# Weights in the free parts of the last inputs' tiles, a tenth pair in another order, and one unit of token products behind the last sum

## The chip, the cores and the metric

The kernel runs on one core of one Trainium2 chip. The metric is the device time of one execution in microseconds (us); the median of three runs stands for the kernel.

## What is computed

Two layers follow each other. The first is linear attention with a decay: for each of 4 batches and 8 heads a 64x64 state is decayed and added to at each of 768 positions. Its output, 3072 tokens of 512 numbers, goes into a soft mixture of experts: 32 slots take a softmax-weighted mean of all tokens, 8 experts of 4 slots each run two matrix products, and each token takes a softmax-weighted mean of the 32 slot outputs.

```python
for t in range(S):
    state = gamma * state + einsum('bhd,bhe->bhde', k[:, :, t], v[:, :, t])
    y[:, :, t] = scale * einsum('bhd,bhde->bhe', q[:, :, t], state)
x = y as 3072 tokens x 512
logits = x @ phi                                   # phi 512 x 32
slot_input = softmax(logits over tokens).T @ x     # 32 x 512, 4 slots per expert
h = maximum(slot_input[e] @ w1[e], 0)              # w1[e] 512 x 1024
slot_out[e] = h @ w2[e]                            # w2[e] 1024 x 512
out = softmax(logits over slots) @ slot_out        # 3072 x 512
```

All numbers are float32. w1 and w2 are 16 MB each (1 MB here is 1024 KB), the inputs q, k, v 18 MB, the output 6 MB.

## The kernel before

**Stages.** The attention runs in 24 steps, a step being 128 positions of one batch with all 8 heads, and the steps go in 12 pairs P = 0 to 11 (steps 2P and 2P + 1). In a pair TensorE does these in order: the part of the output that comes from the state (`carry_mm`, L251), the part from within the step (`attend_mm`, L260, with the masked scores as an operand), the state's update (`state_mm`, L288), the turning of the output into token order (`natural_mm`, L304), and the scores of the next pair (`score_mm`, L227). After each come copies or masks out of PSUM on ScalarE and VectorE (`attend_copy`, L276 to L280; `natural_copy`, L311; `score_mask`, L235). GpSimd decays q and v of the next pair (`decay_q`, L212; `decay_v`, L217). Every second pair closes a group of four steps, whose logits and softmax sums are folded into the pooled slot inputs; `turn_mm` (L364) and `turn_copy` (L369) are part of that.

Then `hidden` (L607) multiplies the slot inputs with the 16 tiles of w1 in the order of the table `weights`, and the last loop (L687) sums the products with w2 in three blocks of output columns, 256, 128 and 128 wide, in 16 units each. A block's sum is finished by the generator `finish`: a copy of the sum to SBUF (`os_`, L652), a product that repeats it for four row groups (L656), a copy of that (`s4`, L657), and then the token products in units of 64 columns: four products (L668), four copies on VectorE and ScalarE in turn (L673), one store of 768 KB (L674). The block of 256 has four such units, the others two each. `finish` is advanced by one `yield` per unit of the next block; the tables Y1, Y2 and BURST say how many yields stand before and between its parts.

**Queues and order.** Every engine runs its instructions in the order of the code. All loads and stores are issued by SyncE (SP): an issue waits until the buffer that it fills has been read for the last time, and what stands behind it in the code waits with it. Every eighth DMA shares a semaphore lane, so an issue also waits until the one eight before it has landed.

**Buffers.** Tiles of 1 MB come from two pools: `big` (13) for weights and `inp` (6) for the inputs of six steps. A step's tile holds kT, qT, v and k in natural order, 512 columns of the 2048 each. Steps in LEAN load only the first three (768 KB) and make the fourth on TensorE where it is wanted; the last four steps, 20 to 23, don't want it, since no state follows them. `load_in(2P + 6)` and `(2P + 7)` are issued in pair P, so the last inputs (22, 23) are issued in pair 8. PACE gives the number of weight tiles issued in each pair: 13 up to P = 8, which fills `big`; two in P = 10 and two in P = 11, which go into the tiles of steps 18 to 21 once those are done. In P = 11 follow the first half tile of w2 in a slot of `ring` and a second in `sst` (the state), and two tiles in those of steps 22 and 23. Four more halves go to the ring, and the last ten tiles take the place of w1 tiles that `hidden` has used.

Of the kernel before, what the change touches and what calls it, by code (L numbers as in the profile page):

```python
# [34 lines left out]
BURST = (3, 3, 3)  # L35
BLOCKS = [(0, 256), (256, 128), (384, 128)]
Y1 = (3, 3, 1)
Y2 = (4, 4, 1)
# [6 lines left out]
PACE = (1, 1, 1, 2, 1, 2, 1, 2, 2, 0, 2, 2)  # L45
# [36 lines left out]
def retention_soft_moe_kernel(  # L82
# [5 lines left out]
    w2: bass.AP,  # L88
    first_: bass.AP,
# [57 lines left out]
    weights = [("w1", hf, g, k) for hf in range(2) for g in range(2) for k in range(NK)]  # L147
    weights += [("w2", 0, e, hf) for hf in range(2) for e in range(0, NE, 2)]
    weights += [("w2", cb, e, 0) for cb in (1, 2) for e in range(0, NE, 2)]

    def halves_of(cb, e, hf):
        if cb == 0:
            return [[(e + h, 4 * hf + f) for f in range(4)] for h in range(2)]
        return [[(e + h, fc) for fc in range(NFC)] for h in range(2)]

    def load_weights(n):
        for _ in range(n):
            if not weights:
                return
            which, *at = weights.pop(0)  # L160
            t = large(weight_pool[0])
            if which == "w1":
                nc.sync.dma_start(t, w1[tuple(at)])
                w1t[tuple(at)] = t
            else:
                nc.sync.dma_start(t, w2[w2n[0]])
                w2n[0] += 1
                take(at, [t[:, 0:1024], t[:, 1024:2048]])

    def take(at, tiles):  # L170
        w = BLOCKS[at[0]][1]
        for t, fcs in zip(tiles, halves_of(*at)):
            for x, (e, fc) in enumerate(fcs):
                w2t[e, at[0], fc] = t[:, x * w:(x + 1) * w]

    def load_halves(n, first_half=None):
        for _ in range(n):
            _, *at = weights.pop(0)
            tiles = [first_half if first_half is not None else slot(), slot()]
            for h in (1, 0):  # L180
                nc.sync.dma_start(tiles[h], w2[w2n[0], :, h * 1024:(h + 1) * 1024])
            take(at, tiles)
            w2n[0] += 1
# [4 lines left out]
    def load_in(i):  # L188
        t = large(inp)
        st[i] = dict(kT=t[:, 0:512].rearrange("p (g t) -> p g t", t=C),  # L190
# [170 lines left out]
    def turn_mm(g):  # L361
        q = gs[g]
        q["tp"] = bank("sm", (128, C))
        nc.tensor.transpose(q["tp"], q["pT"], ident)  # L364
# [100 lines left out]
    for P in range(NPP):  # L465
        last = P == NPP - 1
        g = P // 2
        load_weights(PACE[P])
        if 2 * P + NIN < NSTEP:
# [42 lines left out]
        if 2 * P + 2 in TURNED:  # L512
            turn_k(2 * P + 2, "A0")
        natural_mm(P)
# [13 lines left out]
        if P == NPP - 2:  # L528
            logits_bank(NGRP - 1)
# [8 lines left out]
        if P % 2 == 0 and 0 < P < NPP - 2:  # L538
# [12 lines left out]
    load_halves(1)  # L551
# [17 lines left out]
    load_halves(1)  # L569
# [34 lines left out]
    def hidden(hf, g, k):  # L604
        for j in range(4):
            a = g * NK * SIW + k * SIW + 4 * j
            nc.tensor.matmul(hp[hf][32 * j:32 * j + 32, :], si0[:, a:a + NSLOT],  # L607
                             w1t[hf, g, k][:, j * 512:(j + 1) * 512],
# [18 lines left out]
    for hf in range(2):  # L627
        for g2 in range(2):
            for k in range(NK):
                hidden(hf, g2, k)  # L630
                load_weights(1)
# [9 lines left out]
    load_weights(len(weights))  # L641

    co_tags = [["sm", "A2", "Y1", "A3", "S", "A0", "Y0"], ["sm", "A2", "Y1", "A3", "S", "A1", "Y0"]]
    last_tags = ["S", "sm", "A2", "Y1", "A3", "A1", "A0", "Y0"]
    pend = []
    n_co = [0]

    def finish(cb, op):
# [11 lines left out]
        for m in range(w // 128):  # L660
            for h in range(2):
                ot = large(big)[:, 0:12 * C].rearrange("p (c j t) -> p c j t", j=B, t=C)
                cps = []
                for j in range(B):
                    tags = co_tags[cb] if cb < len(BLOCKS) - 1 else last_tags
                    cp = bank(tags[n_co[0] % len(tags)]).rearrange("p (c t) -> p c t", t=C)[:, 0:3]
                    n_co[0] += 1
                    nc.tensor.matmul(cp, s4[32 * j:32 * j + 32, m * 128:(m + 1) * 128],  # L668
                                     cT[32 * j:32 * j + 32, 3 * h:3 * h + 3, :], start=True, stop=True,
                                     skip_group_check=True, tile_position=(32 * j, 0))  # L670
                    cps.append(cp)
                for j in range(B):
                    (nc.scalar.copy if j % 2 else nc.vector.tensor_copy)(ot[:, :, j, :], cps[j])  # L673
                nc.sync.dma_start(out[c0 + m * 128:c0 + (m + 1) * 128, h * 12 * C:(h + 1) * 12 * C],  # L674
                                  ot.rearrange("p c j t -> p (c j t)"))
                for _ in range(BURST[cb]):
                    yield

    for cb, (c0, w) in enumerate(BLOCKS):
        if cb == len(BLOCKS) - 1:  # L680
            n_co[0] = 0
# [13 lines left out]
        next(done)  # L695
        for f in pend:
# [7 lines left out]
def lay_out(q, k, v, moe_phi, moe_w1, moe_w2):  # L704
# [16 lines left out]
    for cb, (c0, w) in enumerate(BLOCKS):  # L721
# [3 lines left out]
        else:  # L725
            x = x.reshape(NE // 2, 2, NFC, 128, w).transpose(0, 3, 1, 2, 4)
        w2.append(x.reshape(-1, 128, 2 * FF))
    kt, qt, vn = tr(k), tr(q), nat(v)
    x = np.concatenate([kt, qt, vn, nat(k)], axis=2)
    return dict(x3=x[LEAN][:, :, 0:1536], x4=x[FULL],  # L730
                w1=w1, w2=np.concatenate(w2),
# [24 lines left out]
```

## Time and profile before

| | us |
|---|---|
| median of 3 runs | 158.79 (158.37 to 158.86) |
| profiled execution, its device time | 159.76 |
| its span, first to last instruction | 158.1 |
| TensorE busy in it | 143.1 |
| VectorE, GpSimd, ScalarE busy | 77.6, 58.3, 43.9 |
| read from and written to HBM | 55.05 MB and 6.29 MB (of 10^6 bytes) |

The profiled execution took 159.76 us, 1.7 more than its span; the shown runs without a profile have a median of 158.79. TensorE's granted clock was 1.00 of full speed up to 152 us. The time axis of all rows starts with the span.

### The profile page before, as it was taken

Reading aid. Unit: us, or ns where it says so; the run is one execution under the profiler, and the core shown is the slowest. Engines: PE = TensorE matmul, PEld = TensorE weight load, DVE = VectorE, ACT = ScalarE, POOL = GpSimd, SP = SyncE. Lnnn points to the kernel's source line nnn. Section 1 sums busy time; section 2 is a strip of 40 time slices with the busy share of each in tenths; the row PEclk is TensorE's granted clock in tenths of the full one; section 3 lists DMA queues with packets and bytes.
Section 4 is the critical chain, followed back from the end, with each engine's and each line's share of the span. In section 5 each row is a group of like instructions: output and inputs, shape, how many; then the busy total and the mean of one; then the engine's idle time right before and its main releaser. Section 6 shows DMA issues by size and latency. Waiting matters only on the chain.

```text
span 158.1 us, 5523 instructions
## 1 busy us (share of the span) xinstructions
PE 143.1 (91%) x2424; PEld 106.8 (68%) x2424; DVE 77.6 (49%) x187; ACT 43.9 (28%) x104; POOL 58.3 (37%) x67
## 2 busy tenths in 40 slices
PE   7989999999999798999989997999999999998400
PEld 2769999997999587997979796865333565556200
DVE  0349517483847376574937583766410103545500
ACT  3212452415062303423142205150500001423400
POOL 1352798686838059911994093001100000000000
PEclk9999999999999999999999999999999999999975
DMA  4999999999999999999999978989999999999992
GB/s 174 349 418 435 416 417 418 411 426 417 417 412 419 417 409 424 390 423 417 409 426 401 326 311 309 411 286 424 417 430 413 423 423 419 415 407 421 422 418 95
DMA packets 9816, 61.70 MB, mean 390 GB/s; under 512 B 1088, under 2 KB 1088, under 8 KB 4928
## 3 DMA queue, kind: packets, MB, share of 16 engines
q1 hardware_dynamic: 9792, 61.35, 95.2%
q8 instruction: 19, 0.31, 0.8%
q14 instruction: 5, 0.04, 0.1%
HBM read 55.05 MB, written 6.29 MB: 388 GB/s over the span
## 4 chain that ended last, share of the span: by engine, by line
PE 83%; DMA 5%; POOL 2%; DVE 2%; issue 1%; SPq 1%; ACT 1%; DVEq 0%; ACTq 0%
PE A L227 13%; PE Y L260 13%; PE A L687 9%; PE A L304 7%; PE S L288 6%; PE Y L251 6%; DMA b<-in_x_dram 5%; PE Y L607 4%; PE A L607 4%; PE sm L328 3%; PE A L206 3%; PE S L384 3%; PE S L668 2%; POOL b L212 2%; PE A L668 2%
## 5 line engine op out<-in xcount | busy, mean ns | idle before, releaser
L235 DVE TENSOR_TENSOR r<-A,mi 128x512 f32<-128x512 f32 (+1 forms) x50 | 30.1, 661 | 23.9 <-PE A L227 23.9
L212 POOL TENSOR_TENSOR b<-b,qtab 128x512 f32<-128x512 f32 x20 | 25.3, 1277 | 9.3 <-DMA b<-in_x_dram 4.2
L227 PE MATMUL A<-b 64*128 64x128 f32 x384 | 25.7, 283 | 0.7 <-DMA b<-in_x_dram 0.6
L227 PEld LDWEIGHTS A<-b 64*128 64x128 f32 x384 | 23.0, 191 | 3.9 <-issue 1.7
L217 POOL TENSOR_TENSOR b<-b,kt 128x512 f32<-128x512 f32 x23 | 23.7, 1048 | 3.6 <-DMA b<-in_x_dram 3.6
L260 PE MATMUL Y<-r,b 128*64 128x128 f32 x352 | 21.9, 276 | 0.7 <-POOL b L212 0.7
L260 PEld LDWEIGHTS Y<-r,b 128*64 128x64 f32 x352 | 19.0, 137 | 2.7 <-issue 1.7
L430 POOL TENSOR_TENSOR cn<-cn,cz 128x128 f32<-128x128 f32 x6 | 2.4, 400 | 36.6 <-DVE zc L404 18.5
L687 PE MATMUL A<-b,r 128*32 128x128 f32 (+1 forms) x336 | 14.6, 301 | 0.1
L687 PEld LDWEIGHTS A<-b,r 128*32 128x32 f32 x336 | 9.4, 109 | 6.7 <-issue 4.4
L311 ACT COPY r<-A 128x512 f32<-128x512 f32 x23 | 12.5, 595 | 5.2 <-PE A L304 5.2
L304 PE MATMUL A<-mi,r 128*128 128x128 f32 x96 | 12.9, 276 | 0.8 <-ACT r L279 0.8
L288 PE MATMUL S<-b 128*64 128x64 f32 x304 | 11.1, 222 | 1.3 <-issue 1.3
L304 PEld LDWEIGHTS A<-mi,r 128*128 128x128 f32 x96 | 10.6, 141 | 1.7 <-ACT r L279 1.1
L288 PEld LDWEIGHTS S<-b 128*64 128x64 f32 x304 | 10.4, 138 | 1.6 <-issue 1.6
L251 PE MATMUL Y<-b,sst 64*64 64x128 f32 x304 | 10.6, 276 | 0.0
L280 DVE COPY r<-Y 128x512 f32<-128x512 f32 x9 | 6.2, 691 | 5.9 <-PE Y L260 5.1
L251 PEld LDWEIGHTS Y<-b,sst 64*64 64x64 f32 x304 | 8.2, 132 | 1.2
L297 DVE TENSOR_TENSOR sst<-sst,S 128x256 f32<-128x256 f32 x16 | 6.0, 417 | 3.5 <-PE S L288 3.5
L673 ACT COPY b<-A 128x384 f32<-128x384 f32 x8 | 3.7, 484 | 14.4 <-PE A L668 12.8
L607 PE MATMUL Y<-b,qtab 128*32 128x512 f32 x64 | 7.3, 594 | 0.0
L351 ACT ACTIVATE pT<-sm,nm 128x128 f32<-128x128 f32 x4 | 1.5, 368 | 20.8 <-PE Y L260 10.5
(143 smaller groups left out, 184.0 us busy)
## 6 DMA issues: line engine op xcount, KB each, us to landing
b<-in_w_dram SPq DMA_DIRECT2D x29, 1024.0 KB, 13.3
b<-in_x_dram SPq DMA_DIRECT2D x14, 768.0 KB, 9.3
b<-in_x_dram SPq DMA_DIRECT2D x9, 1024.0 KB, 10.4
out_dram<-b SPq DMA_DIRECT2D x8, 768.0 KB, 9.0
r<-in_w_dram SPq DMA_DIRECT2D x5, 512.0 KB, 9.8
b<-in_first_dram SPq DMA_DIRECT2D x1, 512.0 KB, 3.4
r<-in_first_dram SPq DMA_DIRECT2D x1, 512.0 KB, 4.3
sst<-in_w_dram SPq DMA_DIRECT2D x1, 512.0 KB, 5.7
```

The costliest lines, as they stand in the source:

```text
L212: nc.gpsimd.tensor_tensor(q, q, qtab, ALU.mult)
L217: nc.gpsimd.tensor_tensor(v, v, vsc[:, i // B, a:b].unsqueeze(2).broadcast_to([128, b - a, D]), ALU.mult)
L227: nc.tensor.matmul(s["sc"][r][:, g, :], s["kT"][half(r), g, :], s["qT"][half(r), g, :], start=True, stop=True, skip_group_check=True)
L235: nc.vector.tensor_tensor(s["A"][:, r, g:g + n], s["sc"][r][:, g:g + n], mask.unsqueeze(1).broadcast_to([128, n, C]), ALU.mult)
L251: nc.tensor.matmul(p["y"][k][b][half(half_of(r, g)), gl, :], sst[(2 * P + k) % B][half(r), g, :], s["qT"][half(r), g, :], start=(gl == 0 a ...
L260: nc.tensor.matmul(pr[P]["y"][k][g // 2][half(half_of(r, g)), g % 2, :], s["v"][:, 2 * g + r, :], s["A"][:, r, g, :], start=(P < B // 2 an ...
L288: nc.tensor.matmul(S_[half(r), k, g, :], s["kn"][:, 2 * g + r, :], s["v"][:, 2 * g + r, :], start=True, stop=True, skip_group_check=True)
L304: nc.tensor.transpose(X[k][:, g * 128:(g + 1) * 128], pr[P]["yT"][:, k, g, :], ident)
L311: (nc.scalar.copy if engines[k] == "scalar" else nc.vector.tensor_copy)(xn, pr[P]["X"][k])
L607: nc.tensor.matmul(hp[hf][32 * j:32 * j + 32, :], si0[:, a:a + NSLOT], w1t[hf, g, k][:, j * 512:(j + 1) * 512], start=(g == 0 and k == 0), ...
L668: nc.tensor.matmul(cp, s4[32 * j:32 * j + 32, m * 128:(m + 1) * 128], cT[32 * j:32 * j + 32, 3 * h:3 * h + 3, :], start=True, stop=True, s ...
L687: nc.tensor.matmul(op[32 * j:32 * j + 32, :w], hT[fc // 4][:, fc % 4, 4 * g + j, :], w2t[4 * g + j, cb, fc], start=(n == 0), stop=(n == le ...
```

## The change

It does four things. First, each of the last four steps' tiles gets a quarter of another kind: the columns 1536 to 2047, unused in these steps, are loaded with 256 KB of w2 (`wq`) right behind the step's own input. Second, the first three quarters of the same four tiles are filled with w2 (`wl`, 768 KB each) after the step is done, in the place where whole tiles were loaded. w2's first 4 MB are laid out in HBM for that; the sixteenth tile of w1 comes in two halves, one into a ring slot in P = 10, the other into `sst`. The bytes are the same as before. Third, pair 10 has an order of its own: the scores of step 22 come ahead of `turn_mm` and `natural_mm`, which use other PSUM banks. Fourth, the second unit of token products of the second block (column block 1) is no longer worked off in the third block's loop; its products come after the third block's sum, behind that sum's repeating product, and its copies behind the copy `s4`.

```diff
-BURST = (3, 3, 3)
+BURST = (3, NFC * 2, 1)
+HELD = (1, 1)
-Y1 = (3, 3, 1)
-Y2 = (4, 4, 1)
+Y1 = (3, 3, 2)
+Y2 = (4, 4, 2)
-PACE = (1, 1, 1, 2, 1, 2, 1, 2, 2, 0, 2, 2)
+PACE = (1, 1, 1, 2, 1, 2, 1, 2, 2, 0, 2, 0)
...
+    def load_last_w1(h, t):
+        nc.sync.dma_start(t, w1[1, 1, NK - 1, :, h * 1024:(h + 1) * 1024])
+        w1t.setdefault((1, 1, NK - 1), []).extend(t[:, j * 512:(j + 1) * 512] for j in range(2))
+
+    def load_behind(i):
+        m = i - (NSTEP - B)
+        t = st[i]["tile"][:, 0:1536]
+        nc.sync.dma_start(t, wl[m])
+        take(early[8 + 6 * m:14 + 6 * m], t)
...
         elif i in LEAN:
             nc.sync.dma_start(t[:, 0:1536], in3[LEAN.index(i)])
+            if i >= NSTEP - B:
+                m = i - (NSTEP - B)
+                nc.sync.dma_start(t[:, 1536:2048], wq[m])
+                take(early[2 * m:2 * m + 2], t[:, 1536:2048])
...
         load_weights(PACE[P])
+        if P == NPP - 2:
+            load_last_w1(0, slot())
+        if last:
+            load_behind(2 * P - 2)
+            load_behind(2 * P - 1)
...
         carry_mm(P)
         if last:
-            load_halves(1, sall)
-            load_weights(2)
+            load_last_w1(1, sall)
         attend_mm(P)
         if last:
+            load_behind(2 * P)
+            load_behind(2 * P + 1)
             break
...
+        if P == NPP - 2:
+            score_mm(2 * P + 2)
+            score_mask(2 * P + 2)
+            turn_mm(g - 1, "A2")
+            turn_copy(g - 1)
+            natural_mm(P, names=("S", "sm"))
+            natural_copy(P)
+            logits_bank(NGRP - 1)
+            score_mm(2 * P + 3)
+            score_mask(2 * P + 3)
+            continue
...
+            if (cb, u) == HELD:
+                yield
+            for j in range(B):
+                (nc.scalar.copy if j % 2 else nc.vector.tensor_copy)(ot[:, :, j, :], cps[j])
...
         done = finish(cb, op)
         next(done)
+        if cb == len(BLOCKS) - 1:
+            next(pend[0])
+            next(done)
         for f in pend:
             for _ in f:
                 pass
```

SP's queue behind the input of step 20 stood like this before; x3 are inputs (steps 21, 22, 23), w1 and w2 weights, b a tile of 1 MB, r a ring slot:

```order
L199 DMA b_1055<-in_x3_dram 128x1536
L163 DMA b_1205<-in_w1_dram 128x2048
L163 DMA b_1207<-in_w1_dram 128x2048
L199 DMA b_1209<-in_x3_dram 128x1536
L199 DMA b_1211<-in_x3_dram 128x1536
L163 DMA b_1463<-in_w1_dram 128x2048
L163 DMA b_1465<-in_w1_dram 128x2048
L163 DMA b_1553<-in_w1_dram 128x2048
L166 DMA b_1555<-in_w2_dram 128x2048
L181 DMA r_1577<-in_w2_dram 128x1024
L181 DMA sst_81<-in_w2_dram 128x1024
```

The same place now, from the first quarter of w2 on:

```order
L213 DMA b_1053<-in_wq_dram 128x512
L210 DMA b_1056<-in_x3_dram 128x1536
L213 DMA b_1056<-in_wq_dram 128x512
L170 DMA b_1207<-in_w1_dram 128x2048
L170 DMA b_1209<-in_w1_dram 128x2048
L210 DMA b_1211<-in_x3_dram 128x1536
L213 DMA b_1211<-in_wq_dram 128x512
L210 DMA b_1214<-in_x3_dram 128x1536
L213 DMA b_1214<-in_wq_dram 128x512
L170 DMA b_1467<-in_w1_dram 128x2048
L170 DMA b_1469<-in_w1_dram 128x2048
L187 DMA r_1471<-in_w1_dram 128x1024
```

Four quarters (1 MB) and one half tile (0.5 MB) moved ahead of the first issue that needs the tile of step 20 or 21; SP issues 74 DMAs and branches where it had 70.

TensorE at the end of pair 10, from the last attend products on, before (b_1209 is step 22, b_1211 step 23):

```order
L260 MATMUL Y1_1472<-r_1447,b_1055 64x128 x4
L304 MATMUL A2_1508<-mi_75,r_1505 128x128 x4
L304 MATMUL A3_1513<-mi_75,r_1505 128x128 x4
L364 MATMUL sm_1521<-mi_75,pT_1450 128x128
L227 MATMUL A0_1527<-b_1209 128x128
L227 MATMUL A1_1528<-b_1209 128x128
```

The same place now (b_1211 is step 22, b_1214 step 23):

```order
L275 MATMUL Y1_1478<-r_1451,b_1056 64x128 x4
L242 MATMUL A0_1514<-b_1211 128x128
L242 MATMUL A1_1515<-b_1211 128x128
...
L379 MATMUL A2_1527<-mi_75,pT_1454 128x128
L319 MATMUL S_1531<-mi_75,r_1511 128x128 x4
L319 MATMUL sm_1536<-mi_75,r_1511 128x128 x4
L242 MATMUL A2_1546<-b_1214 128x128
L242 MATMUL A3_1547<-b_1214 128x128
```

The scores of step 22 stand where the turning products of pair 10 stood, which read the copied output of that pair.

TensorE at the third block, before: the last 12 products of its first half, the second unit of block 1 (S, A_2083, Y_2085, sm), the second half, the repeating product, the first unit of block 2:

```order
L687 MATMUL A_2030<-b,r 32x128 x12
L668 MATMUL S<-cT,r 128x384
L668 MATMUL A_2083<-cT,r 128x384
L668 MATMUL Y_2085<-cT,r 128x384
L668 MATMUL sm<-cT,r 128x384
L687 MATMUL A_2030<-b,r 32x128 x32
L656 MATMUL Y_2129<-os,rep 128x128
L668 MATMUL S<-cT,r 128x384
```

The same place now; S, A_2121, Y_2123 and A_2125 are the held unit:

```order
L715 MATMUL A_2030<-b,r 32x128 x44
L686 MATMUL Y_2115<-os,rep 128x128
L696 MATMUL S<-cT,r 128x384
L696 MATMUL A_2121<-cT,r 128x384
L696 MATMUL Y_2123<-cT,r 128x384
L696 MATMUL A_2125<-cT,r 128x384
L696 MATMUL sm<-cT,r 128x384
```

The unit moved from the middle of the sum to behind the repeating product (L686), so that three units instead of two follow the sum.

## Rows read from the trace of the kernel before

**Rows 1.** The page, the chain that ended last, by engine.
```profile
PE 83%; DMA 5%; POOL 2%; DVE 2%; issue 1%; SPq 1%; ACT 1%; DVEq 0%; ACTq 0%
```

**Rows 2.** Stretches: window, PE PEld DVE ACT POOL busy (x), clock, DMA share, GB/s.
```profile
92.00:96.00 4.00, 3.17 (x69) 2.69 (x66) 3.43 (x9) 1.11 (x4) 4.00 (x5) 1.00 0.61 215
104.00:108.00 4.00, 4.00 (x49) 2.59 (x48) 3.36 (x11) 1.71 (x7) 0.00 (x0) 1.00 0.84 347
112.00:116.00 4.00, 4.00 (x44) 1.04 (x32) 0.82 (x5) 2.05 (x3) 0.40 (x1) 1.00 1.02 416
```

**Rows 3.** Timeline of SP's issues: start, length until the last issue's end, line, tile, count.
```profile
79.23 1.45 SPq L199 DMA_DIRECT2D b<-in_x_dram  x2
86.88 7.73 SPq L163 DMA_DIRECT2D b<-in_w_dram  x3
95.17 0.33 SPq L166 DMA_DIRECT2D b<-in_w_dram  x1
95.62 0.36 SPq L181 DMA_DIRECT2D r<-in_w_dram  x1
100.29 0.33 SPq L181 DMA_DIRECT2D sst<-in_w_dram  x1
101.34 1.20 SPq L166 DMA_DIRECT2D b<-in_w_dram  x2
102.63 3.07 SPq L181 DMA_DIRECT2D r<-in_w_dram  x4
109.53 11.96 SPq L166 DMA_DIRECT2D b<-in_w_dram  x10
134.70 15.45 SPq L674 DMA_DIRECT2D out_dram<-b  x8
```

**Rows 4.** DMAs issued at 80.35, 94.28, 105.38, 121.16, 149.82; last number: us to landing.
```profile
b<-in_x_dram SPq DMA_DIRECT2D x1, 768.0 KB, 10.0
...
b<-in_w_dram SPq DMA_DIRECT2D x1, 1024.0 KB, 4.7
...
r<-in_w_dram SPq DMA_DIRECT2D x1, 512.0 KB, 10.8
...
b<-in_w_dram SPq DMA_DIRECT2D x1, 1024.0 KB, 21.4
...
out_dram<-b SPq DMA_DIRECT2D x1, 768.0 KB, 7.1
```

**Rows 5.** Timeline at pair 10, PE, ACT, POOL: in brackets idle before, and releaser.
```profile
93.10 1.97 PE L260 MATMUL Y<-r,b 128*64 128x128 f32 x32
95.90 1.09 PE L304 MATMUL A<-mi,r 128*128 128x128 f32 x8 [0.83 <-ACT r L279]
97.03 2.06 PE L227 MATMUL A<-b 64*128 64x128 f32 x32
...
95.27 0.57 ACT L279 COPY r<-Y 128x512 f32<-128x512 f32 x1
...
91.28 2.51 POOL L212 TENSOR_TENSOR b<-b,qtab 128x512 f32<-128x512 f32 x2
```

**Rows 6.** Timeline of the last sum and what follows it, PE and DVE.
```profile
142.76 0.58 PE L668 MATMUL S<-cT,r 32*128 32x384 f32 x1
...
143.62 1.95 PE L687 MATMUL A<-b,r 128*32 128x128 f32 x64
...
146.86 0.58 PE L668 MATMUL S<-cT,r 32*128 32x384 f32 x1 [0.38 <-DVE r L657]
...
145.64 0.29 DVE L652 COPY os<-A 128x128 f32<-128x128 f32 x1 [0.91 <-PE A L687]
146.51 0.29 DVE L657 COPY r<-Y 128x128 f32<-128x128 f32 x1 [0.58 <-PE Y L656]
147.81 0.56 DVE L673 COPY b<-S 128x384 f32<-128x384 f32 x1 [1.00 <-PE Y L668]
148.28 1.48 DVE L673 COPY b<-A 128x384 f32<-128x384 f32 x3
```

More of the change, by code (lines that the diff above doesn't have):

```diff
@@ L146, in retention_soft_moe_kernel, with keys_of, take @@
     w1t, w2t, w2n = {}, {}, [0]
[L147 to L151, printed above, removed]
+    weights = [("w1", hf, g, k) for hf in range(2) for g in range(2) for k in range(NK)][:-1]
+    weights += [("w2", 0, n) for n in range(4, 8)] + [("w2", cb, n) for cb in (1, 2) for n in range(4)]
+    def keys_of(cb, n):
         if cb == 0:
-            return [[(e + h, 4 * hf + f) for f in range(4)] for h in range(2)]
-        return [[(e + h, fc) for fc in range(NFC)] for h in range(2)]
+            return [(2 * (n % 4) + h, 0, 4 * (n // 4) + f) for h in range(2) for f in range(4)]
+        return [(2 * n + h, cb, fc) for h in range(2) for fc in range(NFC)]
+    early = [k for n in range(4) for k in keys_of(0, n)]
+    def take(keys, t):
+        w = BLOCKS[keys[0][1]][1]
+        for x, k in enumerate(keys):
+            w2t[k] = t[:, x * w:(x + 1) * w]
     def load_weights(n):
         for _ in range(n):
-            if not weights:
-                return
             which, *at = weights.pop(0)
@@ L163, in load_weights @@
                 nc.sync.dma_start(t, w1[tuple(at)])
-                w1t[tuple(at)] = t
+                w1t[tuple(at)] = [t[:, j * 512:(j + 1) * 512] for j in range(4)]
             else:
@@ L167, in load_weights, with load_halves @@
                 w2n[0] += 1
[L168 to L183, printed above, removed]
+                take(keys_of(*at), t)
+    def load_halves():
+        _, *at = weights.pop(0)
+        keys = keys_of(*at)
+        for h in range(2):
+            t = slot()
+            nc.sync.dma_start(t, w2[w2n[0], :, h * 1024:(h + 1) * 1024])
+            take(keys[h * len(keys) // 2:(h + 1) * len(keys) // 2], t)
+        w2n[0] += 1
+    def load_last_w1(h, t):
[6 more added lines that the diff above has]
+        take(early[8 + 6 * m:14 + 6 * m], t)
     st = {}
@@ L537, in retention_soft_moe_kernel @@
                 combine_c(g - 1)
-        if P % 2 == 0 and 0 < P < NPP - 2:
+        if P % 2 == 0 and P > 0:
             combine_a(g - 1)
@@ L630, in retention_soft_moe_kernel @@
                 hidden(hf, g2, k)
-                load_weights(1)
+                if weights:
+                    load_weights(1)
                 if (hf, g2, k) == (0, 0, 0):
@@ L640, in retention_soft_moe_kernel @@
                     hidden_t(0)
-    load_weights(len(weights))
-    co_tags = [["sm", "A2", "Y1", "A3", "S", "A0", "Y0"], ["sm", "A2", "Y1", "A3", "S", "A1", "Y0"]]
-    last_tags = ["S", "sm", "A2", "Y1", "A3", "A1", "A0", "Y0"]
+    assert not weights
+    tags = [["sm", "A2", "Y1", "A3", "S", "A0", "Y0"], ["sm", "A2", "Y1", "A3", "S", "A1", "Y1", "A3"],
+            ["sm", "A2", "A0", "Y0", "A1", "A3", "S", "Y1"]]
     pend = []
-    n_co = [0]
     def finish(cb, op):
```

55 lines of the change are left out of this document (26 added, 29 removed).

## The prediction, made before the changed kernel was run

> **What bounds the kernel now.** I read the chain that ended last first. TensorE has 83% of it [rows 1], so at first sight DMAs should not matter. The stretches say otherwise: the transfers run at 416 GB/s in a full stretch, and fall to 215 and 347 GB/s in two earlier ones, 92 to 96 and 104 to 108 [rows 2]. SP's timeline [rows 3] with the time to landing [rows 4] shows what that hole costs at the end. The last of the four half tiles is issued at 105.4 and lands at 105.4 + 10.8 = 116.2. After it come ten weight tiles of 1 MB and eight stores of 768 KB, 16 MB, and the last store lands at 149.8 + 7.1 = 156.9. That is 40.7 us or 2.55 us per MB with no hole. The last weight lands at 121.2 + 21.4 = 142.6, and the half of the last sum that needs it begins at 143.6 [rows 6]. So two things end together: TensorE is 1.0 us behind the weights, and the stores stand in the queue: the last one takes 7.1 us to land, while a tile of 1 MB issued into an empty queue at 94.3 took 4.7 [rows 4]. The queue, not TensorE, sets the last 5 us.
>
> How much the hole costs: the input of step 23 lands at 80.35 + 10.0 = 90.35. From there to 116.2 come 3 + 1 + 0.5 + 0.5 + 2 + 2 = 9 MB [rows 3], 25.85 us where 9 x 2.55 = 22.95 would do: **2.9 us lost**. The cause is in the same rows: the third of the three tiles "from 86.88 on" is issued at 94.28, after SP has waited for the tile of step 18, and the half tile for the state only at 100.29, after `carry_mm` of the last pair.
>
> **The change part by part.** *The hole.* 1.5 MB now stand ahead of the first issue that waits for the tile of step 20: four quarters of 256 KB behind the last inputs and one half tile of w1. At 2.55 us per MB that is 3.8 us of transfers, more than the 2.9 that are missing. Does the queue stay filled? Step 23 has three quarters ahead of it and lands at 90.35 + 1.9 = 92.3; then follow the fourth quarter (92.9), two w1 tiles (98.0), the half (99.3), the pieces behind steps 20 and 21 (101.2, 103.1), the half in the state (104.4), and so on. An empty queue needs 4.7 - 2.55 = 2.15 us from issue to the first byte [rows 4]. The piece behind step 20 is issued at 94.28 and is wanted by 97.1; the state's half is issued at 100.29, or 0.8 earlier by the next part, and is wanted by 100.9. That is the tightest, and it holds. So I take the whole 2.9: the stream could end at 156.9 - 2.9 = **154.0**. SP issues four more DMAs at about 0.4 us, in stretches in which it waits anyway. The issue of the half tile into the ring could hold up the ones behind it (the pieces behind steps 20 and 21); its slot held the masked scores of step 19, used in pair 9, so I cost that wait at nothing. A lane admits eight DMAs at a time; eight of the small ones still hold about 5 MB, 12 us of transfers against the 2.15 needed.
>
> *The price of small rows.* A quarter moves 2 KB per partition. No row of before has that. The nearest has 4 KB: between 112 and 116 only ring halves were landing, and they ran at 416 GB/s [rows 2], full rate. Below, no gain is possible, since nothing runs above full rate; above, a row of 2 KB may take as long as one of 4 KB, which makes the 1 MB cost 5.1 instead of 2.55. Bounds 0 and +2.55; I take 0, the nearer row.
>
> A rule of the Trainium skill speaks against this part: DMA: Bandwidth & Descriptors, in "Anatomy of one DMA", puts a fixed cost of about 2.0 us on each DMA, and in "Measured" asks for at least 1 MiB each. By that, as an estimate, four more DMAs add 8 us, and the kernel would be some 5 us slower. The half tiles of 512 KB at 416 GB/s [rows 2] show no such cost while others are in flight.
>
> *Pair 10.* TensorE ends the attend products at 95.07 and waits 0.83 us, until 95.90, for ScalarE's copy of 95.27 [rows 5]. Now the scores of step 22 stand there, half of 2.06, about 1.0 us, and cover it. They need q of step 22 decayed: GpSimd does both steps' from 91.28 to 93.79 [rows 5], and both inputs have landed by 92.3, before the second is due at 92.5. The scores of step 23 have until 97.2. `turn_copy` comes ahead of two copies on ScalarE, which was idle. Bounds 0 and 0.83; I take **0.8**, since every operand has a us to spare. All of TensorE's later work comes earlier by that.
>
> *The held unit.* It took TensorE from 142.76 to 143.62, **0.86 us** ahead of the last half of the sum [rows 6]. The sum ended at 143.62 + 1.95 = 145.57; now at 145.57 - 0.83 - 0.86 = 143.9, if weights have come. They land at 142.6 - 2.9 = 139.7, used from 141.9 on: yes.
>
> *The tail.* Counted from the sum's end, before: copy `os` at +0.07, copy `s4` from +0.94 to +1.23, first product at +1.29, first copy out at +2.24, 0.95 later; two units' copies take VectorE 1.95, 0.97 each [rows 6]. Now the held unit's products can start right behind the repeating product, about +0.9, so its copies start at +1.85 (VectorE is free at +1.23) and the three units are done at +2.85, +3.8 and +4.75; before, two were done at +3.3 and +4.2. The three stores are issued at about 146.8, 147.7 and 148.7. What is late next: the store of the held unit. The five before it would have landed at 154.0 - 3 x 1.91 = 148.3; its first byte comes at 146.8 + 2.15 = 148.95, so the queue is empty for 0.65. The last store lands at 154.0 + 0.65 = **154.7**.
>
> **Sum.** 156.9 - 154.7 = 2.2 us shorter. The profiled execution of 159.8 becomes 157.6, its span 155.9; it was 1.0 above the median of 158.8, so the forecast is **156.6**.
>
> **The rivals.**
> 1. *Pair 10 gains nothing*, because step 22's scores wait in their new place. The sum ends at 144.7, the held store is issued at 147.65 and the last lands at 155.5: time 157.4. Against it: the decays end 1.3 us before.
> 2. *Half the hole stays*, because an issue behind the half tile or the state is late. Then 1.45 of the 2.9 are kept, the stream ends at 155.45: time 157.3. For it: the state's half is issued only 0.6 to 1.4 us ahead of need.
> 3. *Small rows cost double.* The stream ends at 154.0 + 2.55 = 156.55, and the tail is in time for it: 0.35 shorter, 158.4, which a measurement of this kernel can hardly tell from no change (0.3%, about 0.5 us).
> 4. *Slower.* Place: the queue from step 21's input on. If each of the four additional DMAs pays its first byte alone, 2.15 us as in the empty queue, the stream ends at 154.0 + 8.6 = 162.6, and step 23, behind three of them, lands at 98.7, after its scores are due: time 158.8 + 5.7 = 164.5. It turns the sign from 2.9 / 4 = 0.7 us per DMA on. The full rate of the half tiles [rows 2] is against it.
> 5. *Better.* The queue has no gap ahead of the held store: the stream ends at 154.0, time 155.9.
>
> **How the numbers follow.** Forecast 0.54, rivals 1 to 5: 0.12, 0.12, 0.07, 0.05, 0.10. Faster: 0.54 + 0.12 + 0.12 + 0.10 = 0.88; same 0.07; slower 0.05. The range reaches from 155.4 (rival 5, with 0.5 of the 0.75 that 25 MB at the 416 GB/s of [rows 2], 2.52 instead of 2.55 us per MB, would take off) to 157.9 (rival 2 with a quarter of the doubled rows, 0.6). Rivals 3 and 4 stay out, 0.12.
>
> **What would show it.** Right: no stretch of 2 us between 90 and 146 under 380 GB/s; the last weight lands near 139.7; the pause of 0.83 at pair 10 is gone and TensorE stands 0.8 earlier from there on; the sum ends near 143.9; the three last stores are issued at 146.8 to 148.7 and the last lands near 154.7. Wrong: a quarter's landing that adds more than 0.7 us to that of the DMA ahead of it (rivals 3 and 4); scores of step 22 that wait for GpSimd or a DMA (1); a hole left at 95 or 104 (2). The forecast falls too if the weights, and not the stores, turn out to set the end: a last weight later than 141 delays the sum.

## The result, and the profile after

The changed kernel takes **157.15 us** (median of 6 runs, 155.87 to 157.38) beside 158.82 us for the kernel before in the same comparison; the ratio is 0.9889, with a 95% interval of 0.9843 to 0.9935. A second comparison, of 12 runs beside 35 of the kernel before, gave 156.42 beside 157.80 us, ratio 0.9938 (0.9901 to 0.9975). A ratio is taken from the fast runs alone (those within 1.5% of the fastest of their kernel), so it need not be the quotient of the two medians. So the changed kernel is faster, by 1.8 and 1.0 us by the two ratios and by 1.7 and 1.4 us by the medians. The forecast was 156.6 us, from 158.8.

The profiled execution took 157.36 us (159.76 before), its span is 155.7 us (158.1). Its chain that ended last reads much like the one in [rows 1]:

```profile
PE 87%; DMA 2%; DVE 2%; issue 2%; POOL 2%; DVEq 0%
```

By this view TensorE matters even more than before. The stretches (window, busy time of PE, PEld, DVE, ACT and POOL with counts, clock, DMA share, GB/s), to be laid beside [rows 2], say what has changed and what has not:

```profile
92.00:96.00 4.00, 3.31 (x52) 2.89 (x51) 1.93 (x7) 1.23 (x4) 3.45 (x4) 1.00 0.97 380
100.00:104.00 4.00, 4.00 (x73) 2.88 (x70) 1.85 (x5) 1.97 (x6) 0.00 (x0) 1.00 0.93 244
104.00:108.00 4.00, 4.00 (x47) 2.47 (x47) 3.30 (x12) 1.07 (x4) 0.00 (x0) 1.00 0.96 374
112.00:116.00 4.00, 4.00 (x41) 1.20 (x29) 0.74 (x2) 1.20 (x2) 0.23 (x1) 1.00 1.03 430
144.00:148.00 4.00, 3.35 (x26) 1.72 (x26) 2.88 (x8) 2.23 (x6) 0.00 (x0) 1.00 0.95 391
```

The stretch from 92 to 96 rose from 215 to 380 GB/s, the one from 104 to 108 from 347 to 374. But 100 to 104 fell from 362 (in the profile of before) to 244. A part of the hole was filled and another part has moved 8 us on.

SP's issues (start, length until the last issue's end, line, tile, count), for [rows 3]:

```profile
78.29 0.43 SPq L213 DMA_DIRECT2D b<-in_wq_dram  x1
79.11 0.33 SPq L210 DMA_DIRECT2D b<-in_x_dram  x1
79.70 0.33 SPq L213 DMA_DIRECT2D b<-in_wq_dram  x1
85.37 0.81 SPq L170 DMA_DIRECT2D b<-in_w_dram  x2
86.29 0.37 SPq L187 DMA_DIRECT2D r<-in_w_dram  x1
94.61 0.83 SPq L193 DMA_DIRECT2D b<-in_wl_dram  x2
99.43 0.33 SPq L187 DMA_DIRECT2D sst<-in_w_dram  x1
100.48 1.78 SPq L193 DMA_DIRECT2D b<-in_wl_dram  x2
...
108.68 11.25 SPq L173 DMA_DIRECT2D b<-in_w_dram  x10
133.84 14.99 SPq L704 DMA_DIRECT2D out_dram<-b  x8
```

And the DMAs issued at 78.29, 79.11, 79.70, 99.43, 119.60, 146.59 and 148.44, for [rows 4] (last number: us to landing):

```profile
b<-in_wq_dram SPq DMA_DIRECT2D x1, 256.0 KB, 11.5
...
b<-in_x_dram SPq DMA_DIRECT2D x1, 768.0 KB, 12.5
...
b<-in_wq_dram SPq DMA_DIRECT2D x1, 256.0 KB, 12.6
...
sst<-in_w_dram SPq DMA_DIRECT2D x1, 512.0 KB, 4.9
...
b<-in_w_dram SPq DMA_DIRECT2D x1, 1024.0 KB, 20.5
...
out_dram<-b SPq DMA_DIRECT2D x1, 768.0 KB, 4.6
...
out_dram<-b SPq DMA_DIRECT2D x1, 768.0 KB, 6.4
```

Step 23's input lands at 91.6 and the quarter behind it at 92.3, 0.7 later for 256 KB. The state's half, issued at 99.43, lands at 104.3. The last weight lands at 140.1. The last three stores are issued at 146.59, 147.52 and 148.44 and the last lands at 154.8.

Pair 10 on TensorE and ScalarE, for [rows 5]. The pause of 0.83 us ahead of L304 (now L319) is gone: the scores of step 22 (L242 at 94.95) cover ScalarE's copy. Another idle of 1.04 us, which waits for nothing that the profile shows, stands in `carry_mm` just ahead:

```profile
92.69 0.44 PE L266 MATMUL Y<-b,sst 64*64 64x128 f32 x4 [1.04 <-issue]
93.06 1.97 PE L275 MATMUL Y<-r,b 128*64 128x128 f32 x32
94.95 1.16 PE L242 MATMUL A<-b 64*128 64x128 f32 x16
96.05 0.33 PE L379 MATMUL A<-mi,pT 128*128 128x128 f32 x1
96.21 0.60 PE L319 MATMUL S<-mi,r 128*128 128x128 f32 x4
...
94.63 0.59 ACT L294 COPY r<-Y 128x512 f32<-128x512 f32 x1 [0.76 <-PE Y L275]
```

The end, for [rows 6]: the sum's last products run without a break, the held unit's products begin at 144.56 behind the repeating product, and its first copy at 145.50, behind `s4` (L687):

```profile
141.11 2.61 PE L715 MATMUL A<-b,r 128*32 128x128 f32 x88
144.14 0.49 PE L686 MATMUL Y<-os,rep 128*128 128x128 f32 x2 [0.41 <-DVE os L682]
144.56 0.58 PE L696 MATMUL S<-cT,r 32*128 32x384 f32 x1
...
143.79 0.29 DVE L682 COPY os<-A 128x128 f32<-128x128 f32 x1 [1.57 <-PE A L715]
144.66 0.29 DVE L687 COPY r<-Y 128x128 f32<-128x128 f32 x1 [0.58 <-PE Y L686]
145.50 0.56 DVE L703 COPY b<-S 128x384 f32<-128x384 f32 x1 [0.55 <-PE A L696]
```

### The profile page after: what moved, and what is told of

Same layout as the page of the kernel before. It is cut to its first block, busy times and chain, and to the rows that moved or that the text cites. A ratio compares the mean times of both kernels' runs of the same rounds, so it can differ in the third digit from the quotient of the medians.

```text
span 155.7 us, 5529 instructions
## 1 busy us (share of the span) xinstructions
PE 143.1 (92%) x2424; PEld 106.9 (69%) x2424; DVE 78.1 (50%) x187; ACT 43.9 (28%) x104; POOL 58.7 (38%) x67
## 4 chain that ended last, share of the span: by engine, by line
PE 87%; DMA 2%; DVE 2%; issue 2%; POOL 2%; DVEq 0%
PE A L242 15%; PE Y L275 14%; PE A L715 9%; PE A L319 7%; PE S L303 6%; PE Y L266 6%; PE Y L637 4%; PE A L637 4%; PE sm L343 4%; PE A L221 3%; PE S L399 3%; DMA b<-in_first_dram 2%; POOL b L227 2%; DVE b L703 2%; PE A L696 1%
## 5 line engine op out<-in xcount | busy, mean ns | idle before, releaser
L242 PE MATMUL A<-b 64*128 64x128 f32 x384 | 25.5, 280 | 0.3 <-DMA b<-in_first_dram 0.3
L242 PEld LDWEIGHTS A<-b 64*128 64x128 f32 x384 | 22.6, 187 | 3.6 <-issue 2.0
L715 PE MATMUL A<-b,r 128*32 128x128 f32 (+1 forms) x352 | 14.4, 304 | 0.1
L326 ACT COPY r<-A 128x512 f32<-128x512 f32 x21 | 11.4, 595 | 4.3 <-PE A L319 4.3
L319 PE MATMUL A<-mi,r 128*128 128x128 f32 x88 | 11.8, 276 | 0.0
L319 PEld LDWEIGHTS A<-mi,r 128*128 128x128 f32 x88 | 9.7, 141 | 0.6 <-issue 0.4
L703 ACT COPY b<-A 128x384 f32<-128x384 f32 x10 | 4.4, 483 | 17.2 <-PE A L696 16.2
L696 PE MATMUL A<-cT,r 32*128 32x384 f32 x30 | 7.4, 526 | 0.0
L437 ACT ACTIVATE cn<-cn 128x128 f32<-128x128 f32 x6 | 1.9, 310 | 19.6 <-DVE cn L436 19.6
```

The source lines that it names most:

```text
L242: nc.tensor.matmul(s["sc"][r][:, g, :], s["kT"][half(r), g, :], s["qT"][half(r), g, :], start=True, stop=True, skip_group_check=True)
L319: nc.tensor.transpose(X[k][:, g * 128:(g + 1) * 128], pr[P]["yT"][:, k, g, :], ident)
L326: (nc.scalar.copy if engines[k] == "scalar" else nc.vector.tensor_copy)(xn, pr[P]["X"][k])
L715: nc.tensor.matmul(op[32 * j:32 * j + 32, :w], hT[fc // 4][:, fc % 4, 4 * g + j, :], w2t[4 * g + j, cb, fc], start=(n == 0), stop=(n == le ...
```

## The experiments

Two theories stand against each other. **Queue theory** (the prediction's): the stream of transfers, from the last inputs over 16 MB of weights to the eight stores, sets the end, and TensorE has some us to spare. **TensorE theory**: the chain of waits is to be taken at its word, and what shortens TensorE's work ahead of the last sum (pair 10, 0.83 us, and the held unit, 0.86 us) brings the gain.

### What sets the end in the kernel before

Two edits of the kernel before touch one side alone. The first adds products that nobody uses in front of the w1 products, the second takes a transfer away and leaves TensorE's instructions as they were.

```diff
-    warm(1, "A0")
+    warm(3, "A0")        # b_te1; b_te3: warm(6, "A0")
```
```diff
             which, *at = weights.pop(0)
+            if not weights:              # b_less1: the last tile isn't loaded
+                take(at, last_tile)
+                continue
```

Two more calls:

> The kernel before with two more dummy products on TensorE just ahead of the first hidden product, 0.52 us each in the trace, 1.04 us in all, behind the holes in the stream. Theory Q: no change, within 0.3 us: the last sum and the last store's issue come 1.0 us later, its time to landing falls from 7.1 to about 6.1 us. Theory T: 1.0 us slower.

Measured: 158.39 us beside 158.16, ratio 1.004 (0.9994 to 1.0087). The four additional products (two to a call) take 0.87 us in the trace, less than the 1.04 expected, so 1.0055 would be TensorE theory's ratio, and the interval holds it as well as no change. The last store's landing is as the queue theory has it (6.0 us after its issue at 148.62), but that decides nothing by itself. So five more calls:

> The kernel before, with six pairs... of dummy products instead of one in front of the w1 products: five more calls of the same warming product that the kernel has there already, each about 0.43 us of TensorE (two records of 0.21 us in the trace of the run with two more), so about 2.1 us of TensorE work that nothing uses, put behind the holes of 92 to 108 us and ahead of the last sum. Queue theory (the transfers set the end): the last weight lands where it landed in the kernel before (139.8 to 142.6 us), the last sum ends later by up to 2.1 us less what TensorE waited for weights, the last store is issued later but stands a shorter time in the queue, 5.0 to 5.5 us instead of 7.1; the end moves by 0 to 0.8 us, the ratio stays within 1.000 to 1.005. TensorE theory (the chain with 83% of TensorE sets the end): 2.1 us slower, ratio 1.013.

Measured: 157.84 us beside 158.14, ratio 1.0006 (0.9978 to 1.0034). TensorE theory's 1.013 is out. The dummies stand in the trace (first row: eleven of their twelve products, two to a call, 0.43 us a call), and the last two rows are the last weight, issued at 119.77, and the last store, issued at 150.00:

```profile
106.02 2.55 PE L438 MATMUL A<-const-float32-0.0 128*1 128x256 f32 x11
...
b<-in_w_dram SPq DMA_DIRECT2D x1, 1024.0 KB, 20.1
...
out_dram<-b SPq DMA_DIRECT2D x1, 768.0 KB, 4.6
```

TensorE does 5 x 0.43 = 2.1 us more, and the last store waits in the queue so much less: 4.6 us to landing where it was 7.1 [rows 4]. (It is issued only 0.2 later than in [rows 3] because TensorE had come to pair 10 1.9 us earlier in this execution; the ratio is from executions of both kernels and doesn't hang on that.)

> The kernel before without the load of the last weight tile (1 MB of w2): the products that would use it read the tile before it, so the output is not the reference's. TensorE has the same instructions in the same order. Queue theory: everything that stands behind that load in the queue comes 1 MB earlier, the eight stores among them, so the last store lands about 2.5 us earlier, until the tail's own work binds: the last store is issued at 149.8 at the latest and needs 4.7 us into an empty queue, so between 2.0 and 2.5 us faster, ratio 0.984 to 0.987. TensorE theory: the same work on TensorE, at most the 0.9 us faster that the last half sum might have waited; ratio 0.995 to 1.000.

Measured: 155.45 us beside 158.14, ratio 0.9816 (0.9771 to 0.9861): 2.7 us faster by the medians, 2.9 by the ratio. The last weight, issued at 116.96, and the last store, issued at 147.91:

```profile
b<-in_w_dram SPq DMA_DIRECT2D x1, 1024.0 KB, 20.3
...
out_dram<-b SPq DMA_DIRECT2D x1, 768.0 KB, 4.2
```

One MB less, at 2.5 us per MB, accounts for nearly all of it; the gain lies a little above the 2.0 to 2.5 us expected. In this run the tail is the next bound, as the expectation had it: from 147 to 148 the queue moves only 172 GB/s, and the last store lands 4.2 us after its issue. So 2.1 us of work on the engine that has 83% of the chain cost nothing, and 1 MB of transfers is worth its full price: the queue theory stands for the kernel before.

One view sums it up. From the last weight's landing to the last store's landing it takes nearly the same in every kernel, however late the stores were issued (the eight profiles not shown have 14.7 to 14.9):

| kernel | last store issued | last weight landed | last store landed | difference |
|---|---|---|---|---|
| before | 149.82 | 142.60 | 156.97 | 14.4 |
| before, five more dummies | 150.00 | 139.88 | 154.60 | 14.7 |
| before, last weight not loaded | 147.91 | 137.22 | 152.13 | 14.9 |
| changed | 148.44 | 140.11 | 154.82 | 14.7 |
| changed, second profile | 147.57 | 139.07 | 153.98 | 14.9 |
| weights' parts alone, second profile | 146.74 | 139.41 | 153.82 | 14.4 |

Six MB of stores in 14.4 to 14.9 us are 2.4 to 2.5 us per MB, the full rate. In all fourteen profiles the last landing is that of the last weight plus a constant. A landing is that of the slowest of the 16 DMA engines, though, and the others are not busy throughout: in the second row's kernel the stretch from 148 to 152 has a share of 0.78.

### The parts alone

Each part of the change was put into the kernel before by itself. The weights' parts are the first two of the change; the cut from the changed kernel is, in its core:

```diff
-BURST = (3, NFC * 2, 1)
-HELD = (1, 1)
+BURST = (3, 3, 3)
...
-        if P == NPP - 2:
-            score_mm(2 * P + 2)
-            score_mask(2 * P + 2)
-            turn_mm(g - 1, "A2")
...
-            continue
```

> The kernel before with the weights alone: quarters beside and pieces behind the last four steps' inputs, w1's last tile in two halves; pair 10 and the token products as before. Theory Q (the queue of transfers sets the end, the gain is the hole that is filled): 1.5 to 1.9 us faster, nearly all of what the whole change gave; TensorE's last sum ends where it did, near 145.6, and the last store lands some 1.7 us earlier. Theory T (TensorE's chain sets the end, the gain is its 0.83 us pause and the order of the tail): no change, within 0.3 us, since no TensorE instruction moves.

> The kernel before with the new order of pair 10 alone. TensorE's pause of 0.83 us behind the attend products goes in both theories, and the last sum ends about 0.8 us earlier. Theory Q: the time falls only by what the earlier issue of the state's half takes out of the second hole, 0.3 to 0.8 us. Theory T: 0.8 us faster, and the last store's time to landing as before, 7.1 us, since it is issued and lands 0.8 earlier.

> The kernel before with the held unit of token products alone. Theory Q: no change, within 0.3 us: the sum ends 0.86 us earlier, near 144.7, the last store is issued about 0.35 earlier and lands where it did, its time to landing grows from 7.1 to about 7.5 us. Theory T: 0.35 us faster (0.86 of the sum less 0.5 for the third unit behind it).

| kernel | median, us | before, us | ratio (95%) |
|---|---|---|---|
| weights' parts alone | 157.11 | 158.16 | 0.9943 (0.9910 to 0.9975) |
| pair 10 alone | 157.26 | 158.16 | 0.9980 (0.9940 to 1.0020) |
| held unit alone | 158.04 | 158.16 | 0.9990 (0.9947 to 1.0033) |

The weights' parts make the kernel faster, by 0.4 to 1.4 us: more than the 0.3 that TensorE theory allowed, if narrowly, and not the 1.5 to 1.9 expected. The held unit alone shows no gain, though the 0.35 us of TensorE theory would not show in this interval either; its last store is issued at 147.76, two us ahead of [rows 3] (1.5 of them stood at pair 10 already), and stands in the queue just as long as the one in [rows 4] (row: the store issued at 147.76):

```profile
out_dram<-b SPq DMA_DIRECT2D x1, 768.0 KB, 7.2
```

Pair 10 alone is undecided: the medians are 0.9 us apart, the ratio holds no change as well as 0.6% of gain. Both theories had room for 0.8 us there, so this run doesn't part them.

The changed kernel and the weights' parts alone were run once more beside each other:

> The changed kernel once more, to stand beside the three others of this call, since the times of one kernel scatter by about 1% from run to run. Queue theory: the weights in the free parts of the tiles bring nearly all of the gain; 1.0 to 1.7 us below the kernel before, no more than 0.5 us from the kernel with the weights' parts alone. TensorE theory: the order of pair 10 (0.8) and the held unit (0.86) bring it; 1.0 us or more below the kernel with the weights' parts alone.

> The kernel before with the weights' parts of the change alone, once more, beside the changed kernel. Queue theory: 0.9 to 1.5 us below the kernel before, within 0.5 us of the changed kernel. TensorE theory: within 0.5 us of the kernel before.

Measured: 156.42 us (0.9938, 0.9901 to 0.9975) and 157.11 us (0.9963, 0.9927 to 0.9998), before 157.80. By the ratio the weights' parts gain 0.6 us here, short of the 0.9 to 1.5 expected, and this run by itself doesn't exclude TensorE theory's 0.5; the theories are parted by the runs on the kernel before. The medians differ by 0.7 us, a little more than the 0.5 that queue theory allowed and less than TensorE theory's 1.0; the two intervals overlap for the most part. Pair 10 and the held unit together are worth something between 0 and 0.7 us; the runs don't tell it closer.

### The hole that is left

In the changed kernel the stretch from 100 to 104 moves 244 GB/s. If that is because the state's half (99.43) and the pieces behind it are issued too late, 1 MB issued earlier fills it:

```diff
             load_behind(2 * P - 2)
             load_behind(2 * P - 1)
+            load_halves()
...
     natural_copy(NPP - 1, ks=(0,))
-    load_halves()
```

> The changed kernel, with the first two ring halves of w2 (1 MB) issued right behind the pieces behind steps 20 and 21, in ring slots that are free at about 95 us, and the order of the slots after them shifted accordingly. It aims at the stretch from 100 to 104 us, where the changed kernel moves only 244 GB/s. If the transfers there are missing because they are issued too late (the state's half at 99.4 and the pieces behind steps 22 and 23 at 100.5 and 101.4 us, into a queue that has run dry), the stretch rises over 340 GB/s and the fourth ring half lands at 113.2 to 113.8 instead of 114.6 us, the last weight at 138.8 to 139.4 instead of 140.1. The end then is held by the held unit's store: issued at 146.6, first byte 2.15 later, three stores of 1.91, 154.5, so only 0.3 us better than the changed kernel's 154.8. If the 16 DMA engines are the cause (they drift apart and a restart is slow), the stretch stays under 300 GB/s and nothing lands earlier.

> As the run with the two early halves, but the second unit of block 1 worked off in the loop of block 2, as in the kernel before, so that two stores instead of three are issued behind the last sum. The store of that unit is then in the queue before the sum ends. With the stream ahead by 1 us, the last two stores are issued at about 147.7 and 148.6 us; into an empty queue they land at 147.7 + 2.15 + 2 x 1.91 = 153.7. Queue theory: last landing 153.7 to 154.3, the time 0.4 to 1.1 us below that of the changed kernel, ratio to the kernel before 0.982 to 0.990. TensorE theory: the unit of 0.86 us is back ahead of the sum's end and the time is 0.5 to 0.9 us above that of the changed kernel.

Measured: 156.34 us, ratio 0.9898 (0.9866 to 0.9930), with the held unit, and 156.25 us, ratio 0.9890 (0.9858 to 0.9923), without it. Stretches of the former:

```profile
100.00:104.00 4.00, 4.00 (x71) 2.69 (x71) 2.22 (x8) 2.04 (x7) 0.00 (x0) 1.00 1.02 377
...
144.00:148.00 4.00, 2.64 (x24) 1.14 (x20) 2.99 (x7) 2.49 (x6) 0.00 (x0) 1.00 0.71 291
148.00:152.00 4.00, 0.00 (x0) 0.00 (x0) 0.00 (x0) 0.00 (x0) 0.00 (x0) 0.76 1.02 418
152.00:154.00 2.00, 0.00 (x0) 0.00 (x0) 0.00 (x0) 0.00 (x0) 0.00 (x0) 0.50 0.22 89
```

The cause of the hole was named rightly: 377 GB/s instead of 244, and the fourth ring half lands at 113.1 instead of 114.6. The gain is another matter. Both were run again beside the changed kernel:

> The changed kernel with the first two ring halves of w2 issued 1 MB earlier, once more, beside the changed kernel. Queue theory: the hole of 100 to 104 us is filled in it, which takes up to 1.5 us from the stream, of which the tail lets through 0.3 to 0.9 us: 0.4 to 0.9 us below the changed kernel. TensorE theory: no difference, since TensorE's work and its order are the same.

> As the run with the two early halves, without the held unit, once more. Queue theory: the store of that unit fills the queue's gap ahead of the last two stores, but TensorE's unit is back ahead of the last sum and the last store is issued 0.4 to 1.2 us later; the two cancel within 0.4 us. TensorE theory: 0.5 to 0.9 us slower than the run with the two early halves and the held unit.

Measured: 156.62 us, ratio 0.9950 (0.9912 to 0.9987), and 156.46 us, ratio 0.9940 (0.9903 to 0.9976), where the changed kernel had 156.42 us and 0.9938. So the filled hole gains nothing that these runs can see, and neither version beats the changed kernel. The expectation of 0.4 to 0.9 us was wrong, and TensorE theory's "no difference" right for this one; its 0.5 to 0.9 us between the two versions isn't there. The rows above show a part of the reason: what was gained at 100 is idle again from 144 to 148 (share 0.71), ahead of the held unit's store, issued at 145.74. Without the held unit the share from 144 to 148 is 0.88 and 0.84 in two profiles, but the two stores behind the sum are issued later (148.85 and 148.45 the last), and the time is the same.

Another part stands in the landings. Up to the seventh of the last ten weight tiles the first profile with early halves is 1.1 us ahead of the changed kernel's second one (130.51 against 131.62); at the eighth it is 0.1 ahead (133.97 against 134.11). These tiles land 2.5 us apart, but the eighth took 3.5 to 4.1 us in all four profiles with early halves, and 3.1 and 2.5 in the two of the changed kernel. The transfers from 131.60 to 132.85 in the first profile with early halves show what else moves there (queue, packets, MB, share of the 16 engines):

```profile
q1 hardware_dynamic: 76, 0.50, 98.6%
q8 instruction: 1, 0.02, 5.5%
```

The second row is a load of the program's own code, 16 KB, of which every execution has 19. It takes 1.1 us of one engine (5.5% of 16 engines over 1.25 us). Followed packet by packet, that engine finished its share of the eighth tile last, at 133.53; the fifteen others had theirs by 132.81.

The rest of the reason shows in the second profile of the weights' parts alone, in which TensorE was so early (last store issued at 146.74) that nothing is late at the end:

```profile
148.00:152.00 4.00, 0.00 (x0) 0.00 (x0) 0.00 (x0) 0.00 (x0) 0.00 (x0) 0.62 0.83 344
152.00:154.00 2.00, 0.00 (x0) 0.00 (x0) 0.00 (x0) 0.00 (x0) 0.00 (x0) 0.50 0.11 46
```

From 152 on, a share of 0.11 moves 46 GB/s: 0.11 x 16, or two of the 16 engines on average, still work off their rows of the last store while the others have nothing left. The last store lands at 153.82 there, and at 153.85, 153.95 and 153.98 in the two profiles of the version with early halves (and the held unit) and in the second one of the changed kernel. A landing is that of the last of 16 engines, and bytes that the others move earlier don't bring it forward. By the packets of the trace, thirteen engines are done with the last store by 152.05 in this second profile of the weights' parts and three between 153.14 and 153.49; in the two with early halves thirteen by 152.43 and 152.16, three from 153.27 and 153.41 on. Each of these three has three code loads between 129 and 146 us. The second profile of the changed kernel has three as well, but a less clear picture there (ten by 152.48, six from 152.94 to 153.62). That such loads make single engines late, and that the lag of these engines holds all four at the same time, fits these rows; no run moves or removes a code load, so that much is argued and not shown.

## Why the prediction was right, and which term was not

**What bounds the kernel: right.** It was read from the stretches and SP's rows against the chain of waits, and the runs with more TensorE work (1.0006) and with 1 MB less (0.9816) show it.

**The hole: right in cause, the term mis-sized.** The prediction took 2.9 us lost and expected all of it back. Both halves were too good. On the side of before, 2.9 us belong to one execution. In the five other profiles with the old order of the queue the third tile of [rows 3] is issued at 92.3 to 93.1, not 94.28, since TensorE reached pair 10 earlier in them, and the stretches are better filled. In the run with five more dummies, behind pair 10 and so without influence on this place, SP's issues and two stretches:

```profile
84.82 7.90 SPq L163 DMA_DIRECT2D b<-in_w_dram  x3
93.28 0.63 SPq L166 DMA_DIRECT2D b<-in_w_dram  x1
...
98.41 0.33 SPq L181 DMA_DIRECT2D sst<-in_w_dram  x1
...
92.00:96.00 4.00, 3.16 (x45) 2.75 (x43) 1.56 (x7) 2.36 (x7) 2.29 (x3) 1.00 0.72 272
...
104.00:108.00 4.00, 4.00 (x36) 2.26 (x29) 3.05 (x11) 0.80 (x3) 0.00 (x0) 1.00 1.00 417
```

From the landing of step 20's input to that of the last weight (23.25 MB) the execution shown ahead of the prediction took 63.1 us, the five others 60.9 to 61.3 (with 2.5 added for the tile that one of them leaves out). The changed kernel took 61.1 and 60.1, the weights' parts alone 60.2 and 60.5. So against a typical execution the stream gained about 1 us or less, not 2.9. On the side of after, the hole wasn't closed: from the fourth quarter (92.35) to the fourth ring half (114.57) 8 MB took 22.2 us where 8 x 2.55 = 20.4 would do; 1.8 us are lost, between 100 and 104 for the most part. The step that failed is the one on the state's half, "issued at 100.29, or 0.8 earlier", "wanted by 100.9", "That is the tightest, and it holds". By its own measure it held: the half was issued at 99.43, and its first byte was due, 2.15 later, at 101.6, ahead of the landing of the piece behind step 21 (102.3). Yet it landed at 104.3, 2.0 behind that piece where 0.5 MB take 1.3, and the piece behind step 22, issued 1.05 later, took another 3.1 us for 768 KB, 1.1 too long. (The 2.15 came from a tile issued at 94.28 "into an empty queue"; the tile ahead of it landed only at 95.3.) The reason is that engines run short sooner than landings tell, since a landing is that of the last engine. Two stretches of 1 us in the changed kernel's first profile:

```profile
100.00:101.00 1.00, 1.00 (x24) 1.00 (x20) 0.42 (x1) 0.49 (x2) 0.00 (x0) 1.00 0.73 209
...
102.00:103.00 1.00, 1.00 (x34) 0.80 (x27) 0.04 (x1) 0.48 (x1) 0.00 (x0) 1.00 1.39 213
```

From 100 to 101, still ahead of the landing at 102.3, a share of 0.73 is busy. In the second row the share is over 1 at half the rate, because a packet's time counts where it begins: behind the pause six packets of 6 KB took 1.8 to 2.1 us each, where 0.23 is usual. And 1 MB issued ahead of it fills the stretch.

**The level was right for a reason that the prediction had not seen.** It forecast 157.6 for the profiled execution, which took 157.36, and 156.6 for the median, between the 157.15 and 156.42 of the two comparisons. The 1.0 us by which the profiled execution of before stood above the median was carried over as if it were a constant of profiling. It was 0.2 in the changed kernel. That us was the large hole of that execution: a part of the gain was counted that the median of before, as far as the five other profiles tell, never lost. That both levels came out is luck in this respect.

**Small rows: right.** In the two profiles of the changed kernel the quarters land 0.65 to 0.69 us behind the DMA ahead of them (of the 24 in the other six profiles that have them, one took 0.51 and one 0.92): 2.6 to 2.8 us per MB, full rate within 10%, and under the 0.7 us that the prediction set as the mark of rivals 3 and 4. The Trainium skill's fixed cost of about 2.0 us for each DMA (DMA: Bandwidth & Descriptors, "Anatomy of one DMA", measured there on DMAs that GpSimd issues) isn't seen in these landings, where SP's DMAs stand in the queue behind others; the prediction had put it on SP's. Rivals 3 and 4 fall.

**Pair 10: right in mechanism, not as a term of the end.** The pause of 0.83 us is gone, in both profiles of the changed kernel. In the first profile an idle of 1.04 us in `carry_mm` takes it back; the second hasn't that idle (row: `carry_mm` of pair 10, all 32 products) and TensorE is 0.9 us earlier from there on:

```profile
91.15 1.10 PE L266 MATMUL Y<-b,sst 64*64 64x128 f32 x32
```

What TensorE gains there can reach the end through the issues that wait for it (the pieces behind the steps, the state's half). Between these two profiles it did: the stretch from 100 to 104 has 307 GB/s in the second, and the last store lands 0.84 earlier. Between the two of the weights' parts alone it did not: TensorE is 1.9 us earlier in the second (last store issued at 146.74 for 148.64), the last landing 0.72, and 0.60 of that stood at the landing of step 20's input already. Its stream was 1.4 us ahead at the seventh of the last ten weights, and 0.35 at the tenth.

**The held unit and the tail: right in their times, of little use.** The sum ended at 143.7 (143.9 forecast), the stores were issued at 146.6, 147.5 and 148.4 (146.8, 147.7, 148.7), the last landed at 154.8 (154.7). The gap of 0.65 us that the forecast added ahead of the held store isn't there: some engines run dry (share 0.84 from 147 to 148), but that store lands 1.84 us behind the one before it, like all the others. The last landing is right because two other terms were 0.4 too small each: the last weight (140.1 for 139.7), and what follows it (14.7 us for 14.3). Alone the part brings nothing that shows (0.9990); the store that it hurries was waiting in the queue.

**The criteria of the prediction.** The one on the stretches (none under 380 GB/s between 90 and 146) failed (244, 374); the last weight (140.1 for 139.7), the pause, the sum, the stores and the last landing came within 0.4 us. Rival 2, half the hole stays, at 157.3, describes the queue better than the forecast did; the forecast's own sum came out through an execution of before that was worse than its kind.

## What to carry to other kernels

A chain of waits that is 83% TensorE doesn't say that TensorE sets the end; follow the bytes from the last stall to the last landing, and if they run at full rate throughout, the queue does. Before a stall is counted as gain, ask whether it is as large in a typical execution: where the profiled execution is a us above the median, the stall may be that us. A second cure for the same bound can pay nothing, because the next thing (here the tail's stores and the slowest DMA engines) stands less than a us behind the first: filling the hole at 100 moved 1 MB and not the end. Rate and share are means over 16 engines, and a landing waits for the last of them, so look at what else those engines carry.

## What the runs showed of the hardware that was not expected

- After a queue has run short, the rate stays low while the engines count as busy: 244 GB/s at a share of 0.93 from 100 to 104 in the changed kernel, 307 at 0.98 in its second profile, 284 at 1.00 in the kernel with the held unit alone. In full stretches 1.00 goes with 410 to 430. Single packets right behind the pause take up to 2.1 and 2.2 us in the first two, where 0.23 is usual, and count as busy; why they take so long is open.
- TensorE has idles of 0.2 to 1.0 us that wait for nothing that the profile shows, and not in every execution. All 25 in the fourteen profiles stand ahead of its 851st, 977th, 1355th or 1607th product: whole multiples of 126 apart, while 2424 products, with an operand load (PEld) each, go with 19 code loads, about 128 to a load. Each idle ends 1.2 to 1.6 us after a code load has ended (the 1.04 us shown above, up to 92.69, after one from 90.18 to 91.27). So TensorE seems to wait for its code there; no run tests it. The idles make 1.4 of the 1.9 us that the two profiles of the weights' parts alone are apart at pair 10, and move the issues that wait for TensorE's buffers with it.
- A code load takes about 1 us of one DMA engine (0.9 to 1.1 in nearly all), and the tile that this engine works on can land late by it. In seven of the eight profiles with the weights' parts, the eighth of the last ten weights lands 3.1 to 4.1 us behind the seventh, where 2.5 is usual. In five of the eight profiles the packets can be followed: the engine with the load ends its share of that tile 0.4 to 0.5 us ahead of the tile's landing.
- Single times of one kernel range over 1 to 2% (156.1 to 159.5 us for before in one comparison; a single one of 186.39 us, in the runs with two more dummies, is left aside), so that a gain under 0.6 us can't be told even with 12 runs beside 35.
